# Weight stores moved to ScalarE's queue and a pair of token loads held back, in an attention and MoE kernel

## Chip, cores and metric

The kernel runs on one core of a Trainium2 chip. The metric is device time in microseconds (us) of one execution, taken as the median of several runs; lower is better. The engines are TensorE (PE; its weight loads are listed as PEld), VectorE (DVE), ScalarE (ACT), GpSimd (POOL) and SyncE (SP). DMAs are issued by an engine's own queue: SPq is SP's, ACTq is ACT's.

## The reference

```
scores = q @ k.T / 8 + bias(w1, b1, w2)        # 8 batches, 8 heads, 576 positions, 64 wide
attn = exp(scores - max) / (sum + 1e-9)
x = (attn @ v)  laid out as 4608 tokens x 512
a = x @ moe_w1 ; b = x @ moe_w2                # 512 -> 1024
out = ((a * b) @ moe_w3) @ moe_w_out           # 1024 -> 1024 -> 512
```

All is float32. The MoE matrices arrive as 64-bit floats, seen as pairs of 32-bit integers.

## The kernel before

**Stages.** First a table of position bias is made (L525 to L590), then 32 units of attention run (4 head pairs of 8 batches), then a MoE stage in which moe_w3 and moe_w_out are multiplied into one matrix (`fold`, L694) and the tokens go through six pairs of token blocks. A pair is 768 tokens, held as two column blocks c and d of 384. For each pair the hidden width 1024 is taken in 8 steps of 128 columns (the step is called ft or t).

**Precision.** Each operand is split into a high and a low part in a rounded format and a product is three matmuls: high by high, low by high, high by low.

**First pair and others.** For pair 0 a step multiplies plainly (`plain`, L788): 12 matmuls for a into PSUM tile X and 12 for b into PSUM tile Y, for column block c and then d. There is one X and one Y, so the next product has to wait until the old value is read. ScalarE copies X to SBUF (`gate` with "p", L806); VectorE multiplies Y by that copy (`gate` with "g", L809), which frees Y; both then split the result (L797, L800) and PE multiplies it by the folded matrix (`down`, L844). For the other pairs a scheme with seven products in place of eight is used (`product`, L774), with seven combined weight blocks per step.

**Weights.** Step t's weights are fetched in two halves (`fetch_w`; the DMA is L187, into a tile `wi` with two buffers, so a fetch waits until the one before the last was used up). The conversion is: ScalarE L195 and L199, VectorE L205, L209 and L219 (L219 frees `wi`), and POOL's integer sum L213, called the total below. Over eight steps these are 16 fetches. `sums_w` (L644, L647, L650) forms the combinations, `base_w` (L631, L633) splits the plain blocks; both write the tile `wS` (three buffers). At the end of `sums_w` the whole tile of 1792 KB is stored to DRAM (`w_d`, L652), to be loaded again for each later pair (`load_w`, L656).

**Tokens.** `load_x` fetches, for one half of a pair, two blocks `xr` (L711) and the softmax factors `rb` (L423), in many small DMAs. `split_x` multiplies the two (L734), forms differences (L737) and splits them (L742, L744) for pair 1 and later; `split_x0` does it for pair 0 (L722, L724, L726). `xr` and `rb` have one buffer each, so the loads of one half wait for the half before it.

**What sets the order.** From the MoE stage on, the order of PE, ACT, DVE and POOL is written out by hand: each step is put into a list `later` with a due time (in a model's microseconds), and `drive` emits the list in order of these times under a manual schedule for these four engines. SP's order is not in the list: a scheduler decides where each DMA of SP stands, by when it takes the DMA to be ready. Each engine and each queue works strictly in its order, so a DMA that waits holds back what stands behind it on the same queue.

Of the kernel before, what the change touches and what calls it, by code (L numbers as in the profile page):

```python
# [130 lines left out]
def relpos_attention_moe(  # L131
# [17 lines left out]
    nc = tc.nc  # L149
# [11 lines left out]
    def f(ap):  # L161
        return ap.bitcast(F32)
# [80 lines left out]
    def put(plan, steps, *times):  # L243

        def one():
            next(steps, None)
        for at in times:
            plan.append((at, len(plan), one))
# [111 lines left out]
    for i in range(2):  # L360
        t = att.enter_context(tc.tile_pool(name=f"sums{i}", bufs=1)).tile([P, 64], F32, name=f"sums{i}")
# [48 lines left out]
    def load_r(rb, p, rows, h, t0, t1):  # L410
        n = t0
        while n < t1:
            b, j = divmod(n, S)
            e = min(t1, b * S + (512 if j < 512 else S))
            o = rb[rows, n - t0:e - t0]
            if j < 512:
                j += b % 4 * 512
                src = r_m[p][b // 4, h:h + 1, j:j + e - n].broadcast_to([64, e - n])
            else:
                assert e - n == 64  # L420
                src = r_t[p][b // 4].rearrange("(h g b) j -> h b g j", h=2, g=2)[h:h + 1, b % 4].broadcast_to([64, 2, 32])
                o = o.rearrange("p (g j) -> p g j", g=2)
            nc.sync.dma_start(o, src)  # L423
            n = e
# [49 lines left out]
    later = []  # L474
# [5 lines left out]
    later = [e[:3] for e in later]  # L480

    plan = [e for e in later if e[0] < 0.0]
    later = [e for e in later if e[0] >= 0.0]
# [6 lines left out]
    with ExitStack() as pro:  # L490
# [29 lines left out]
        def reach(G):  # L520

            return (G + 1) * GR - 1, S - 1 - G * GR
# [9 lines left out]
        for G in range(NGRP):  # L532
            n = max(reach(G)) + 1
# [60 lines left out]
    later = [e for e in later if e[0] >= t_s]  # L594
# [4 lines left out]
    W2 = 2 * CH  # L599
# [10 lines left out]
    w_d = [dram.tile([P, 14 * 2 * P], F32, name=f"w_d{t}") for t in range(NF)]  # L610
# [5 lines left out]
    def fetch_w(t, m):  # L616

        if m == 0:
            big[t] = bg.tile([P, 4, 2 * P], F32, name="big")
        flat = big[t].rearrange("p s n -> p (s n)")  # L620
        src = (moe_w1, moe_w2)[m].rearrange("(c p) n -> p c n", p=P)[:, :, t * P:(t + 1) * P]
        for step in narrow(cva, src, NC * P, flat[:, m * NC * P:(m + 1) * NC * P], nc.sync, pieces=NC, signed=True):
            step()
            yield

    def base_w(t):
        x, w = big.pop(t), ups[0, t]
        w2 = bg.tile([P, 2, 2 * P], F32R, name="w2k", bufs=3)
        base[t] = (w[:, :, 0], w[:, :, 1], w2, w[:, :, 2])
        for o, y in ((w[:, :, 0:2], x[:, 0:2]), (w[:, :, 2], x[:, 3]), (w2, x[:, 2])):  # L630
            nc.scalar.activation(o[:, 0], y, AF.Copy)  # L631
            yield
            nc.vector.tensor_tensor(o[:, 1], y, f(o[:, 0]), op=ALU.subtract)  # L633
            yield

    def sums_w(t):
        x = big[t]
        w = ups[0, t] = wr.tile([P, 2, 7, 2 * P], F32R, name="wS")
        s = bg.tile([P, 4, 2 * P], F32, name="sums", bufs=1)
        for o, y, z, op in (  # L640
            (s[:, 0], x[:, 2], x[:, 3], ALU.add), (s[:, 2], x[:, 0], x[:, 2], ALU.subtract),
            (s[:, 1], s[:, 0], x[:, 0], ALU.subtract), (s[:, 3], x[:, 1], s[:, 1], ALU.subtract),
        ):
            nc.vector.tensor_tensor(o, y, z, op=op)  # L644
            yield
        for o in (0, 2):
            nc.scalar.activation(w[:, 0, 3 + o:5 + o], s[:, o:o + 2], AF.Copy)  # L647
            yield
        for o in (0, 2):
            nc.vector.tensor_tensor(w[:, 1, 3 + o:5 + o], s[:, o:o + 2], f(w[:, 0, 3 + o:5 + o]), op=ALU.subtract)  # L650
            yield
        nc.sync.dma_start(w_d[t], f(w.rearrange("p h s n -> p (h s n)")))  # L652

    def load_w(p, t):
        w = wr.tile([P, 2, 7, 2 * P], F32R, name="wS")
# [50 lines left out]
    def load_x(p, i, pool):  # L706
        xr = pool.tile([P, 8, CH], F32, name="xr")
        rb = pool.tile([P, 2, W2], F32, name="rb")
        flat = xr.rearrange("p s n -> p (s n)")
        for n, cc in enumerate((i, i + 2)):  # L710
            nc.sync.dma_start(flat[:, n * W2:(n + 1) * W2], x_d[cc][:, p * W2:(p + 1) * W2])  # L711
            for h, rows in enumerate((lo, hi)):
                load_r(rb[:, n], cc, rows, h, p * W2, (p + 1) * W2)
        return xr, rb, flat

    def split_x0(i):
        xr, rb, flat = load_x(0, i, (xs, xs1)[i])
        yield
        x = pairs[0]["x"][i] = x0p.tile([P, 2, 4, CH], F32R, name=f"xB{i}")
        for n in range(2):  # L720
            part, o = flat[:, n * W2:(n + 1) * W2], x[:, :, 2 * n:2 * n + 2].rearrange("p h s n -> p h (s n)")
            nc.vector.tensor_tensor(part, part, rb[:, n], op=ALU.mult)  # L722
            yield
            nc.scalar.activation(o[:, 0], part, AF.Copy)  # L724
            yield
            nc.vector.tensor_tensor(o[:, 1], part, f(o[:, 0]), op=ALU.subtract)  # L726
            yield

    def split_x(p, i):

        xr, rb, flat = load_x(p, i, xs)
        yield
        for n in range(2):
            nc.vector.tensor_tensor(flat[:, n * W2:(n + 1) * W2], flat[:, n * W2:(n + 1) * W2], rb[:, n], op=ALU.mult)  # L734
            yield
        for o, x, y in ((4, 1, 0), (6, 3, 1), (5, 3, 4), (7, 2, 5)):
            nc.vector.tensor_tensor(xr[:, o], xr[:, x], xr[:, y], op=ALU.subtract)  # L737
            yield
        x = xb[(p + 1) % 2].tile([P, 2, 7, CH], F32R, name=f"xS{i}")
        for s in range(7):  # L740
            src = xr[:, s + (s > 0)]
            nc.scalar.activation(x[:, 0, s], src, AF.Copy)  # L742
            yield
            nc.vector.tensor_tensor(x[:, 1, s], src, f(x[:, 0, s]), op=ALU.subtract)  # L744
            yield
        pairs[p]["x"][i] = x
# [128 lines left out]
    for i in range(2 * NF):  # L875
        hf, t = divmod(i, NF)
        t0 = t_f - (2 * NF - i) * PACE_F
# [15 lines left out]
    for t in range(NF):  # L893
        t0 = t_f + STEP0 * (t - 3) - LEAD_W * max(0, 3 - t)
        for m, (at0, d) in enumerate((((2.70, 3.35, 3.40, 3.80, 4.10, 4.90), -7.0), ((7.00, 7.65, 7.70, 8.00, 8.40, 9.40), -0.8))):
            size, rest, clamp, shift, mark, total = at0
            put(later, fetch_w(t, m), t0 + d, *(t0 + d for d in (size, rest, clamp, shift, mark, total)))
        t0 += STEP0
        put(later, base_w(t), *(t0 + d for d in (5.40, 6.00, 6.05, 6.55, 6.60, 7.00)))
        put(later, sums_w(t), *(t0 + 4.30 + 0.42 * d for d in range(4)), *(t0 + 9.70 + 0.65 * d for d in range(4)), t0 + 12.45)  # L900
    for i in range(2):
        t0 = t_s + AT_X0 + PACE_X0 * i
        put(later, split_x0(i), t0 - 5.0, *(t0 + d for d in (0.0, 1.1, 2.2, 3.3, 4.4, 5.5)))

    def start(n):
        return t_f + STEP0 * min(n, NF) + STEP * max(n - NF, 0)

    for n in range(NPR * NF):
        p, ft = divmod(n, NF)
        t0, t1 = start(n), start(n + 1)  # L910
        cs = dict(at=(p, ft))
        if p == 0:
            for j, u in AT_U.items():
                for m in range(2):
                    at(t0 + u + 2.08 * m, plain, cs, j, m)
                for k, d in AT_G.items():
                    if n == 0 and k + j == "gc":
                        d = AT_GC
# [18 lines left out]
        elif 0 < p < NPR - 1 and ft in (2, 5):  # L937
            i = int(ft > 4)
# [87 lines left out]
```

## Time and profile before

| what | value |
|---|---|
| median of 3 runs | 1067.21 us (1062.53 to 1070.43) |
| profiled execution | 1070.71 us, of which the span from first to last instruction is 1068.9 |
| PE busy | 1041.3 us, 97% of the span |
| PE weight loads | 828.4 us, 77% |
| DVE busy | 777.1 us, 73% |
| ACT busy | 559.9 us, 52% |
| POOL busy | 318.8 us, 30% |
| mean granted PE clock | 0.992 of full speed |

Times in the profile count from the start of the span. Busy time of PE includes its pipelining, so neighbouring matmuls overlap a little in the list. A releaser in brackets ("<-") is the engine and line whose end ended the idle time before an instruction.

### The profile page before, as it was taken

The page shows a single profiled execution, that of the slowest core. Times are in us where ns is not written, and L with a number is a line of the kernel's source. Part 1 is how long each engine was busy: PE and PEld are TensorE (multiplying, and loading weights), DVE is VectorE, ACT ScalarE, POOL GpSimd, SP SyncE. Part 2 cuts the span into 40 slices and gives each one's busy share as a digit, 9 for nine tenths or more (in the row PEclk, how much of TensorE's full clock was granted, in tenths as well). Part 3 has the DMA queues.
Part 4 walks back from the last instruction along what each step waited for, and adds up shares of the span by engine and source line. Part 5 has one row for each costly group of instructions (what it writes and reads, how often), then busy time and mean ns, then how long its engine had stood idle before and what let it go on. Part 6 is the DMA issues. An engine that isn't in the chain of part 4 may idle for free.

```text
span 1068.9 us, 33609 instructions
## 1 busy us (share of the span) xinstructions
PE 1041.3 (97%) x13968; PEld 828.4 (77%) x13968; DVE 777.1 (73%) x1478; ACT 559.9 (52%) x1277; POOL 318.8 (30%) x342
## 2 busy tenths in 40 slices
PE   7989999999999999999999999999999999999998
PEld 2346666666666666688899999999999999999997
DVE  8989999999999999998887455444635545453333
ACT  6957877886887778856543332323333232332222
POOL 0026885883788388674220000000000000000000
PEclk9979999999999999999999999999999999999999
DMA  7977777777776765367757765565575565545331
GB/s 218 297 237 207 205 199 215 221 213 198 207 223 189 208 190 168 112 175 245 261 197 274 255 220 195 198 246 197 181 262 188 190 234 214 196 183 214 139 138 59
DMA packets 97241, 218.37 MB, mean 204 GB/s; under 512 B 22592, under 2 KB 47296, under 8 KB 90944
## 3 DMA queue, kind: packets, MB, share of 16 engines
q1 hardware_dynamic: 96656, 216.19, 62.4%
q8 instruction: 110, 1.80, 0.7%
q14 instruction: 43, 0.35, 0.1%
q10 hardware_dynamic: 432, 0.02, 0.0%
HBM read 171.45 MB, written 44.71 MB: 202 GB/s over the span
## 4 chain that ended last, share of the span: by engine, by line
PE 79%; DVE 9%; issue 5%; DMA 3%; ACT 2%; SPq 2%; DVEq 0%; ACTq 0%
PE X L774 16%; PE acc L438 12%; PE Y L774 12%; PE s L342 11%; PE oc L844 9%; PE od L844 9%; DVE ts L353 4%; DVE pt L388 3%; PE bacc L562 3%; PE X L788 3%; PE Y L788 3%; DMA wi<-in_moe_w_dram 1%; SPq L423 1%; ACT pp L378 1%; DMA nb_d<-bev 1%
## 5 line engine op out<-in xcount | busy, mean ns | idle before, releaser
L438 PE MATMUL acc<-pt,v 32*64 32x128 f32 (+1 forms) x9216 | 215.4, 295 | 4.5 <-issue 4.3
L438 PEld LDWEIGHTS acc<-pt,v 32*64 32x64 f32 x9216 | 161.2, 131 | 72.8 <-issue 53.1
L378 ACT ACTIVATE pp<-ts,mx 128x576 f32<-128x576 f32 x256 | 196.0, 766 | 40.2 <-DVE mx L353 39.4
L342 PE MATMUL s<-k,q 64*128 64x288 f32 (+1 forms) x1280 | 196.3, 446 | 7.3 <-DVE mx L353 5.2
L774 PE MATMUL X<-xS,wS 128*128 128x384 f32 x960 | 194.9, 338 | 0.0
L353 DVE CUSTOM_DVE_ANT_0 ts<-s,nb 128x576 f32<-128x576 f32 x256 | 182.4, 738 | 7.2 <-PE s L342 7.1
L388 DVE STREAM_TRANSPOSE pt<-pp 128x1152 f32<-128x1152 f32 x128 | 175.5, 1373 | 3.0 <-ACT pp L378 2.5
L774 PEld LDWEIGHTS X<-xS,wS 128*128 128x128 f32 x960 | 171.4, 188 | 7.0 <-ACT wos L821 0.2
L342 PEld LDWEIGHTS s<-k,q 64*128 64x128 f32 (+1 forms) x1280 | 91.1, 177 | 77.0 <-issue 33.8
L817 DVE TENSOR_TENSOR wos<-X,wos 128x384 f32<-128x384 f32 x80 | 44.6, 558 | 138.7 <-PE X L774 138.7
L774 PE MATMUL Y<-xS,wS 128*128 128x384 f32 x720 | 145.0, 336 | 0.0
L774 PEld LDWEIGHTS Y<-xS,wS 128*128 128x128 f32 x720 | 127.9, 188 | 0.1
L330 POOL COPY v<-v 64x512 f32<-64x512 f32 (+1 forms) x160 | 87.6, 567 | 124.1 <-DMA v<-in_v_dram 109.2
L821 ACT COPY wos<-X 128x384 f32<-128x384 f32 x80 | 38.5, 481 | 126.1 <-PE X L774 126.1
L797 ACT ACTIVATE ghd<-wos 128x384 fp32r<-128x384 f32 x48 | 25.2, 525 | 125.4 <-DVE wos L817 105.7
L844 PE MATMUL oc<-w3s,ghc 128*128 128x512 f32 x288 | 89.8, 393 | 0.0
L844 PE MATMUL od<-w3s,ghd 128*128 128x512 f32 x288 | 89.6, 392 | 0.0
L817 DVE TENSOR_TENSOR wos<-Y,wos 128x384 f32<-128x384 f32 x80 | 44.6, 558 | 50.1 <-ACT wos L821 36.7
L225 POOL TENSOR_TENSOR wmag<-wmag 128x512 int32<-128x512 int32 x72 | 74.9, 1040 | 5.8
L797 ACT ACTIVATE ghc<-wos 128x384 fp32r<-128x384 f32 x48 | 25.2, 525 | 92.5 <-DVE wos L817 75.6
L844 PEld LDWEIGHTS oc<-w3s,ghc 128*128 128x128 f32 x288 | 53.4, 188 | 8.6
L844 PEld LDWEIGHTS od<-w3s,ghd 128*128 128x128 f32 x288 | 53.5, 188 | 8.5
(99 smaller groups left out, 1400.3 us busy)
## 6 DMA issues: line engine op xcount, KB each, us to landing
wS<-w_d SPq DMA_DIRECT2D x40, 1792.0 KB, 7.6
q<-in_q_dram SPq DMA_DIRECT2D x64, 288.0 KB, 4.3
w_d<-wS SPq DMA_DIRECT2D x8, 1792.0 KB, 6.5
v<-in_v_dram SPq DMA_DIRECT2D x96, 128.0 KB, 4.1
nb_d<-bev SPq DMA_DIRECT2D x36, 295.5 KB, 4.1
k<-in_k_dram SPq DMA_DIRECT2D x64, 144.0 KB, 4.0
x_d<-x SPq DMA_DIRECT2D x32, 288.0 KB, 3.8
xr<-x_d SPq DMA_DIRECT2D x24, 384.0 KB, 4.4
```

Source lines behind the costliest of these rows:

```text
L225: nc.gpsimd.tensor_tensor(d["bits"], d["bits"], d["bits"], op=ALU.add)
L330: nc.gpsimd.tensor_copy(t[64:128], t[0:64])
L342: nc.tensor.matmul(s[outs, hf, :HS], d[f"q{h}"][rows, q0:q0 + n], d[f"k{h}"][rows, :], start=True, stop=True,)
L353: nc.vector.tensor_tensor_reduce(out=halves(ts), in0=d.pop(("s", t))[:, :, :HS], in1=halves(NB[p, t]), op0=ALU.add, op1=ALU.min, scale=-1. ...
L378: nc.scalar.activation(d["p", ps][:, k * S:(k + 1) * S], ts, AF.Exp, bias=mx, scale=-1.0, accum_out=SUMS[u // 4 % 2][:, col:col + 1],)
L388: nc.vector.transpose(o, st[u].pop(("p", ts)))
L438: nc.tensor.matmul(acc[outs, a, c0:c0 + 32 * (t1 - t0)], d["v", b][rows, h], pt_[rows, t0:t1, 32 * b:32 * b + 32], start=(b == 0), stop=(b ...
L774: nc.tensor.matmul(acc, w[:, l, W_AT[n], i * P:(i + 1) * P], x[:, r, X_AT[n]], start=(k in "125" and i == 0 and m == 0), stop=(i == 1 and ...
L788: nc.tensor.matmul(acc, w[:, l, i * P:(i + 1) * P], x[:, r, 2 * k + "cd".index(j)], start=(n == 0), stop=(n == 11),)
L797: nc.scalar.activation(st[n], st["g" + j], AF.Copy)
L817: nc.vector.tensor_tensor(st[o], x, y, op=op)
L844: nc.tensor.matmul(d["o", j, t], l[:, sl], folded[ft][r], start=(ft == 0 and n == 0), stop=(ft == NF - 1 and n == 2),)
```

## The change

Three edits. The store of the split up weights is issued by ScalarE instead of SyncE. As ScalarE's order is written out by hand, the store's due time in `sums_w` now counts: it was t0 + 12.45 and becomes t0 + 19.50, 21.00 and 16.50 for step 0, step 1 and the later steps. And for the first half of pair 1 `load_x` has POOL clear two columns of `xr` and one column in 64 of `rb` before the loads are issued, so that each of these loads has to wait for POOL to reach this place in its order; the loads overwrite what was cleared.

```diff
-        nc.sync.dma_start(w_d[t], f(w.rearrange("p h s n -> p (h s n)")))
+        nc.scalar.dma_start(w_d[t], f(w.rearrange("p h s n -> p (h s n)")))
...
         flat = xr.rearrange("p s n -> p (s n)")
+        if (p, i) == (1, 0):
+            nc.gpsimd.memset(flat[:, 0:2 * W2:W2], 0.0)
+            nc.gpsimd.memset(rb.rearrange("p n (s j) -> p (n s) j", j=64)[:, :, 0:1], 0.0)
...
-        put(later, sums_w(t), *(t0 + 4.30 + 0.42 * d for d in range(4)), *(t0 + 9.70 + 0.65 * d for d in range(4)), t0 + 12.45)
+        put(later, sums_w(t), *(t0 + 4.30 + 0.42 * d for d in range(4)), *(t0 + 9.70 + 0.65 * d for d in range(4)), t0 + (19.50, 21.00, 16.50)[min(t, 2)])
```

Three lines are added at L710, so a line of the old kernel beyond it has a number three higher in the new one (L711 becomes L714, L806 becomes L809 and so on).

On SP's queue, at the start of pair 0's products, the old order is this (`wi` is a weight fetch, `xr` and `rb` from x_d_88, r_m_92 and r_t_96 belong to pair 1's first half, `w_d` is the store):

```order
L187 DMA wi<-in_moe_w_dram 128x4x256 x2
L711 DMA xr<-x_d_88 128x768
L652 DMA w_d_8994<-wS 128x3584
L187 DMA wi<-in_moe_w_dram 128x4x256
L423 DMA rb<-r_m_92 64x320
L423 DMA rb<-r_t_96 64x2x32
L423 DMA rb<-r_m_92 64x384
L423 DMA rb<-r_m_92 64x320
L187 DMA wi<-in_moe_w_dram 128x4x256
L652 DMA w_d_8995<-wS 128x3584
L187 DMA wi<-in_moe_w_dram 128x4x256
```

In the new order the same place of SP's queue reads:

```order
L187 DMA wi<-in_moe_w_dram 128x4x256 x12
L714 DMA xr<-x_d_88 128x768
L423 DMA rb<-r_m_92 64x320
L423 DMA rb<-r_t_96 64x2x32
L423 DMA rb<-r_m_92 64x384
L423 DMA rb<-r_m_92 64x320
L423 DMA rb<-r_t_96 64x2x32
L423 DMA rb<-r_m_92 64x384
L714 DMA xr<-x_d_90 128x768
```

The fourth to the fifteenth fetch now stand in one row, then come the two `xr` and twelve `rb` loads of pair 1's first half, then the sixteenth fetch. Further on, the weight load of pair 1's step 0 (L656), which stood behind the two `xr` loads of pair 1's second half, now stands ahead of them.

On ACT, around the second store (w_d_8995), the new order is as follows; `X` and `Y` are the PSUM tiles of pair 0, `wacc` those of the fold:

```order
L195 ACTIVATE wmag<-wi 128x512
L199 ACTIVATE big<-wi 128x512
L701 ACTIVATE w3s_1_9713<-wacc_9512 128x512
L652 DMA w_d_8995<-wS 128x3584
L631 ACTIVATE wS<-big 128x512
L701 ACTIVATE w3s_1_9723<-wacc_9516 128x512
L631 ACTIVATE wS<-big 128x256
L809 COPY wos_9741<-X 128x384
L631 ACTIVATE w2k<-big 128x256
L195 ACTIVATE wmag<-wi 128x512
```

The row with the DMA is new, the others stand as before. Eight such rows are added on ACT.

On POOL, near the end of its work, the new order is this; the row with x9 and the one with x3 are the last twelve totals of the weights:

```order
L683 TENSOR_TENSOR w3s_1_9529<-w3s_1_73,w3h 128x512
L683 TENSOR_TENSOR w3s_1_9556<-w3s_1_75,w3h 128x512
L213 TENSOR_TENSOR big<-big,wmag 128x512 x9
L711 MEMSET xr 128x2
L712 MEMSET rb 128x24
L213 TENSOR_TENSOR big<-big,wmag 128x512 x3
```

The two memsets stand behind the thirteenth of the sixteen totals. The orders of PE and DVE are unchanged.

## Rows read from the trace of the kernel before

**Rows 1.** What PE waited for: us in total, times, longest us.
```profile
PE X L788 <- ACT wos L806: 2.2, 1, 2.2
```
**Rows 2.** PE's timeline around 510: start us, us, engine, line, operation, count [idle before <-releaser].
```profile
510.00 3.81 PE L788 MATMUL X<-xB,wS 128*128 128x384 f32 x12 [2.22 <-ACT wos L806]
513.65 1.22 PE L788 MATMUL Y<-xB,w2k 128*128 128x384 f32 x6
```
**Rows 3.** Stretches of 2 us: us, busy of the engines, PEclk, DMA share, GB/s.
```profile
510.00:512.00 2.00, 2.00 (x6) 2.00 (x7) 2.00 (x5) 0.00 (x0) 0.00 (x0) 0.50 0.62 180
```
**Rows 4.** The chain that ended last, around 500 to 510: start us, us, what.
```profile
500.75 7.58 DMA wi<-in_moe_w_dram
...
509.58 0.38 ACT wos L806
```
**Rows 5.** ACT's timeline, 498 to 509.
```profile
498.81 0.63 ACT L631 ACTIVATE wS<-big 128x512 fp32r<-128x512 f32 x1 [1.23 <-POOL big L213]
...
502.13 0.42 ACT L631 ACTIVATE wS<-big 128x256 fp32r<-128x256 f32 x1 [2.20 <-POOL big L213]
...
508.36 0.67 ACT L195 ACTIVATE wmag<-wi 128x512 f32<-128x512 f32 x1 [1.40 <-DMA wi<-in_moe_w_dram]
```
**Rows 6.** The page's DMA issues: count, KB each, median us to landing.
```profile
wS<-w_d SPq DMA_DIRECT2D x40, 1792.0 KB, 7.6
...
w_d<-wS SPq DMA_DIRECT2D x8, 1792.0 KB, 6.5
```
**Rows 7.** DVE's timeline, 496 to 513.
```profile
496.94 2.39 DVE L650 TENSOR_TENSOR wS<-sums,wS 128x512 fp32r<-128x512 f32 x2
...
502.13 0.76 DVE L644 TENSOR_TENSOR sums<-big 128x256 f32<-128x256 f32 x2 [1.40 <-POOL big L213]
...
512.78 0.55 DVE L809 TENSOR_TENSOR wos<-Y,wos 128x384 f32<-128x384 f32 x1
```
**Rows 8.** All waits between 440 and 640, columns as in rows 1.
```profile
PEld Y L788 <- DVE wos L809: 0.3, 1, 0.3
```
**Rows 9.** SP's timeline at 499.
```profile
499.36 0.34 SPq L652 DMA_DIRECT2D w_d<-wS  x1
```
**Rows 10.** The instructions of L187, the weight fetches.
```profile
DMA to landing us min/median/max: 3.5/3.9/8.3
```
**Rows 11.** What SP's queue waited for between 440 and 640, columns as in rows 1.
```profile
SPq L187 <- DVE big L219: 35.0, 11, 5.4
```
**Rows 12.** Groups of POOL's instructions: busy us, mean ns | idle before.
```profile
L362 POOL MEMSET sums<- 128x64 f32 x2 | 0.2, 152 | 0.3 <-POOLq L1011 0.3
```
**Rows 13.** POOL's timeline at 541.
```profile
541.75 1.28 POOL L213 TENSOR_TENSOR big<-big,wmag 128x512 int32<-128x512 int32 x1 [5.47 <-DVE big L219]
```
**Rows 14.** SP's timeline, 564 to 573.
```profile
564.05 1.24 SPq L423 DMA_DIRECT2D rb<-r_m  x2
...
572.60 1.65 SPq L711 DMA_DIRECT2D xr<-x_d  x2
```
**Rows 15.** ACT's timeline, 552 to 558.
```profile
552.55 0.66 ACT L199 ACTIVATE big<-wi 128x512 f32<-128x512 uint32 x1
...
557.05 0.67 ACT L195 ACTIVATE wmag<-wi 128x512 f32<-128x512 f32 x1
```
**Rows 16.** DVE's timeline, 558 to 582.
```profile
558.56 0.42 DVE L205 TENSOR_SCALAR wmag<-wmag 128x512 f32<-128x512 f32 x1
...
562.80 0.55 DVE L809 TENSOR_TENSOR wos<-Y,wos 128x384 f32<-128x384 f32 x1
...
581.64 1.82 DVE L734 TENSOR_TENSOR xr<-xr,rb 128x768 f32<-128x768 f32 x2
```
**Rows 17.** PE's timeline, 561 to 564.
```profile
561.79 2.28 PE L788 MATMUL X<-xB,wS 128*128 128x384 f32 x12
563.91 1.21 PE L788 MATMUL Y<-xB,w2k 128*128 128x384 f32 x6
```
**Rows 18.** The chain that ended last, at 589; columns as in rows 4.
```profile
589.19 2.11 PE Y L788 x12
```

## The prediction

> **What bounds the kernel now.** I read the list of what TensorE waits for first, since PE is busy for 97% of the span: what can be won is what it waits. Its longest entries belong to the bias and attention stages, which the change does not touch. The MoE stage has one: the plain product into PSUM tile X waits 2.2 us for ScalarE's copy at L806 [rows 1]. Then I looked that place up in PE's own timeline. X starts at 510.00 after 2.22 us of idleness and takes 3.81 us for 12 matmuls [rows 2]; the same 12 take 2.28 us elsewhere [rows 17], so another 1.53 us goes after the wait. The stretch table says why: the granted clock is 0.50, the lower level of 1.2 GHz, in 510 to 512 [rows 3], right after PE had stood still. So 2.22 + 1.53 = 3.75 us is all that this place can give, 0.35% of the run.
>
> The chain of waits says who holds L806 back: the weight fetch issued at 500.75 takes 7.58 us, two ScalarE conversions wait for it, and the copy, which stands behind them in ScalarE's order, ends at 509.96 [rows 4]. ScalarE's timeline has the same as 1.40 us of idleness ahead of the conversion at 508.36 [rows 5]. A usual weight fetch lands in 3.9 us [rows 10]. This one (the eighth of sixteen) stands in SP's queue directly behind the store of split up weights that left at 499.36 [rows 9], and a store takes 6.5 us [rows 6]. So the slow fetch is the store's doing.
>
> Last I asked what PE would meet next, and this decides the forecast. After X comes Y, at 513.65 [rows 2]. It needs VectorE's L809, which reads the old Y out of PSUM. L809 stands at 512.78 and ends at 513.33 [rows 7]; the wait list has a weight load of Y waiting 0.3 us for it [rows 8]. VectorE has no idle time at all between the L644 at 502.13, which waited for POOL, and the end of L809 [rows 7]. So L809 is late by VectorE's own work, and an earlier weight fetch does not move it.
>
> **The change part by part.**
>
> *The stores leave from ScalarE.* Eight DMA issues go from SP to ACT. The same store takes SP 0.34 us to issue [rows 9]; for ACT I take 0.4 each, 3.2 us in all. The seven other than store 1 stand, by the order, just ahead of an instruction that idles for POOL, PE or VectorE, or between two that do, and ACT is busy for 52% only. Bounds: 0, and 0.4 for one that finds no idle time; I take 0.
>
> Store 1 matters. It may not leave before VectorE's L650 has written the last of its data: 496.94 + 2.39 = 499.33 [rows 7]. ACT reaches the new place after an L701 and idles there before L631 anyway; it would now wait until 499.33, issue, and start L631 at about 499.75, not 498.81 [rows 5]: 0.94 later. Queued behind it on ACT are L701, L631 and the first L806. The next L631 waits 2.20 us for POOL until 502.13 [rows 5], so the 0.94 is swallowed before anything PE wants. Bounds: 0 to 0.94; I take 0.
>
> The point is that store 1 leaves at the same moment as before (499.36 then, about 499.4 now), 1.3 us ahead of the eighth fetch, which still waits for the same VectorE instruction to free its buffer. Only the queue is another one. What two queues do to each other the trace does not show, since every large transfer of before is on SP's queue. Bounds from rows: unhindered, the fetch lands at 500.75 + 3.9 = 504.65; hindered as now, at 508.33. A slower landing than now I exclude to within some tenths, for no bytes are added.
>
> By the Trainium skill (DMA: Bandwidth & Descriptors, Issuing engines are not separate DMA queues) the queues of all issuing engines run on the same 16 DMA engines, and a second issuer saves only issue time; the same page (Queues, rings and completion order) lets each engine take turns between queues packet by packet. No run here shows two loaded queues. By the first the landing stays near 508.3 and the sum here is 0; by turns in equal bytes it comes forward and the sum is that of the first rival.
>
> Take either end. If nothing changes, PE resumes X at 510.00 as before. If the fetch lands early, ACT is free at 508.36 - 1.40 = 506.96, and its chain of 1.60 us (508.36 to 509.96) ends at 508.56. X then runs from 508.6 to 510.9, and Y still waits for 513.33. Y starts 513.65 - 513.35 = 0.3 us earlier than before. So this part gives 0 to 0.3 us, not 3.75. I take 0.2.
>
> *SP's queue without the stores.* All fetches from the 4th to the 15th now stand in a row. In the old run SP waited 35.0 us in eleven of these fetches for VectorE's L219 [rows 11], which frees the buffer, so they were not late by what stood ahead of them and don't move. 0.
>
> *The loads of the second pair held back.* Two POOL memsets of 2 and 24 columns: 0.15 us each by the nearest row [rows 12], on an engine that idled 5.47 us before the 13th total [rows 13]. They stand behind this total, which ends at 541.75 + 1.28 = 543.03. Two xr and twelve rb loads follow on SP at 0.64 us each (1.24 us for two and the gaps) [rows 14]: 543.3 + 14 x 0.64 = 552.3. VectorE first needs them behind the L205 of 558.56 [rows 16]. The sixteenth weight fetch now stands behind these fourteen, leaves at 552.3 and lands at 556.2 with the usual 3.9 us. ACT wants it at 557.05 [rows 15]. So 0, with 0.85 us in hand before anyone waits. If this cover goes, see the second rival.
>
> *The second half of the pair.* Its two xr loads left at 572.60 [rows 14]; now a weight load of 7.6 us [rows 6] stands ahead in SP's queue. At worst they come 7.6 us later, at 572.60 + 7.6 + 3.9 = 584.1 if the 3.9 us of a 512 KB fetch [rows 10] stand for one of 384 KB, against a first use at 581.64: 2.5 us late. The two products would end at 583.46 + 2.5 = 586.0 and the L809 behind them (0.55) at 586.5 [rows 16]; PE wants its Y at 589.19 [rows 18]. So 2.7 us stay in hand: 0.
>
> **Sum.** -0.2 (Y) and nothing else: the profiled execution's 1070.71 becomes 1070.5. The three times of before are 1062.53 to 1070.43 with median 1067.21; the profiled one lies 3.5 above it. On the median's footing the forecast is 1067.0. A difference of 1% (10.7 us) is about what a measurement of this kernel tells from no change, and the runs themselves spread by 8 us, so this counts as no change.
>
> **Rivals.**
>
> *The wait moves from X to Y and takes the slow clock with it* (slightly slower). If the fetch lands early, PE idles 0.8 us ahead of X and about 2.4 us ahead of Y. The row shows a fall to 0.50 after 2.22 us of idleness; the same after Y's wait costs 1.53. X no longer pays its 1.53, and Y starts 0.3 earlier: net -0.3 + 1.5 = +1.2, so 1068.4. For it: the same length of wait. Against: it needs the two queues to share well.
>
> *The sixteenth fetch comes late* (slower). Place: PE's Y at 563.91 [rows 17]. The fetch leaves at 552.3 and store 5 leaves ACT right behind the fifteenth conversion, which ended at 552.55 + 0.66 = 553.2 [rows 15]: they run side by side. The slowest fetch beside a store took 8.3 us [rows 10]: landing at 560.6. Slack: ACT's L195 would end 557.72 and VectorE's L205 started at 558.56 [rows 15, 16], 0.84; L809 ended 563.35 and Y began 563.91 [rows 16, 17], 0.56. So from a landing after 557.05 + 1.40 = 558.45 on PE waits, at 8.3 us for 2.15 us, plus 1.53 if the clock falls: +3.7, so 1070.9. For it: fourteen issues ahead. Against: this fetch leaves some 0.9 us ahead of the store, the slow ones left behind it.
>
> *The whole 3.75 us goes* (faster): 1063.5. This needs VectorE to bring L809 forward by 3 us. For it: ACT and DMA are freer. Against: VectorE has no gap to close before L809.
>
> *The change doesn't do what it says*: a store that leaves at the same moment and a queue that shares badly give exactly the old trace, 1067.2. It falls together with the forecast.
>
> **Chances.** No change to within a microsecond, 0.50; the wait moves to Y, 0.22; the late sixteenth fetch, 0.15; the whole gain, 0.08; a stall of over 10 us among the reordered loads, for which no row speaks, 0.04; rounding 0.01. Range: from the whole gain at 1063.5 to the late fetch at 1070.9, widened by about 1.3 us on each side because three runs of the same kernel already spread by 8: 1062.2 to 1072.2. Faster by over 1% would need more than every wait PE has in this stage: 0.02. Slower by over 1%: 0.04. Within: 0.94.
>
> **What would show it.** Right: the fetches from the 4th on leave at VectorE's pace; store 1 leaves at about 499.4; L809 ends near 513.3 and Y starts within 0.3 us of it; after that PE waits for nothing; xr loads leave near 543 and the sixteenth fetch lands before 558. Wrong: L809 several microseconds earlier (the whole gain was there), a new PE wait near 564 or 589 (late loads), or a landing of the eighth fetch later than 508.3.

## The result and the profile after

The changed kernel takes 1073.96 us (median of 12 runs, 1071.30 to 1078.20), the kernel before 1067.57 us on the same chips (12 runs, 1062.53 to 1071.43). The ratio is 1.0053, with a 95% interval of 1.0037 to 1.0069: slower by 5.7 us (4.0 to 7.4). That is within 1%, but above the range of the prediction, which ended at 1072.2.

The profiled execution after took 1071.4 us with a span of 1069.5, only 0.7 us more than the profiled one of before. To compare the two one has to go by stages. First the source views of the last attention product, of the plain product and of the product of the later pairs, of the kernel before:

```profile
L438 PE MATMUL acc<-pt,v x9216: 264/294/522, 69.5 to 456.8; 32*64 32x160 f32 x99, 32*64 32x128 f32 x98
L788 PE MATMUL X<-xB,wS x192: 332/338/688, 498.9 to 595.1; 128*128 128x384 f32 x192
L774 PE MATMUL X<-xS,wS x960: 333/337/444, 600.5 to 1060.4; 128*128 128x384 f32 x192
L774 PE MATMUL Y<-xS,wS x720: 333/334/346, 599.5 to 1057.2; 128*128 128x384 f32 x180
```

And the same of the changed kernel:

```profile
L438 PE MATMUL acc<-pt,v x9216: 264/294/523, 68.7 to 452.4; 32*64 32x160 f32 x102, 32*64 32x128 f32 x95
L791 PE MATMUL X<-xB,wS x192: 334/338/446, 494.4 to 595.8; 128*128 128x384 f32 x192
L777 PE MATMUL X<-xS,wS x960: 332/337/346, 601.2 to 1061.0; 128*128 128x384 f32 x192
L777 PE MATMUL Y<-xS,wS x720: 333/334/444, 600.1 to 1057.8; 128*128 128x384 f32 x180
```

"a to b" is the first and last start. The attention, which the change doesn't touch, ended 4.4 us earlier in this execution (452.4 against 456.8; over the runs of this study it ends between 450.7 and 457.9), and this hides the loss. The stage of pair 0, from the first plain product to the first product of pair 1, grew from 599.5 - 498.9 = 100.6 us to 600.1 - 494.4 = 105.7 us: 5.1 us. The five pairs behind it take 1060.4 - 599.5 = 460.9 us before and 1061.0 - 600.1 = 460.9 after. So the loss is in the stage of pair 0, and 5.1 fits the measured 5.7 (4.0 to 7.4).

What PE waited for between 440 and 1080, where before had 2.2 us in one wait [rows 1] and a weight load of 0.3 [rows 8]:

```profile
PE Y L791 <- DVE wos L812: 4.4, 3, 1.5
PE X L791 <- ACT wos L809: 3.0, 2, 1.7
```

Five waits stand at three places. The first is the one that the change was aimed at [rows 2]; PE's timeline there:

```profile
502.39 1.22 PE L791 MATMUL Y<-xB,wS 128*128 128x384 f32 x6
505.30 2.38 PE L791 MATMUL X<-xB,wS 128*128 128x384 f32 x12 [1.68 <-ACT wos L809]
509.22 1.32 PE L791 MATMUL Y<-xB,w2k 128*128 128x384 f32 x6 [1.54 <-DVE wos L812]
```

The X wait is shorter (1.68 against 2.22), its 12 matmuls no longer run at half clock (2.38 against 3.81), and Y waits 1.54 instead. VectorE's timeline says for what, as [rows 7] did:

```profile
497.96 0.76 DVE L644 TENSOR_TENSOR sums<-big 128x256 f32<-128x256 f32 x2 [1.41 <-POOL big L213]
...
508.63 0.54 DVE L812 TENSOR_TENSOR wos<-Y,wos 128x384 f32<-128x384 f32 x1
```

Between these two rows VectorE has no idle time. L812 ends at 509.17, and Y starts at 509.22. In the kernel before the last products into the old Y stand here:

```profile
506.55 1.23 PE L788 MATMUL Y<-xB,wS 128*128 128x384 f32 x6
```

From there to the new Y at 513.65 [rows 2] it was 7.10 us. Now it is 509.22 - 502.39 = 6.83: 0.27 us less.

The second and third places are new. PE's timeline at both, with an undisturbed product in the last two rows:

```profile
557.23 0.39 PE L847 MATMUL od<-w3s,gld 128*128 128x512 f32 x1
558.93 2.38 PE L791 MATMUL X<-xB,wS 128*128 128x384 f32 x12 [1.32 <-ACT wos L809]
562.82 1.31 PE L791 MATMUL Y<-xB,w2k 128*128 128x384 f32 x6 [1.51 <-DVE wos L812]
...
565.03 0.63 PE L847 MATMUL oc<-w3s,ghc 128*128 128x512 f32 x2
...
585.92 2.28 PE L791 MATMUL X<-xB,wS 128*128 128x384 f32 x12
589.54 1.34 PE L791 MATMUL Y<-xB,w2k 128*128 128x384 f32 x6 [1.33 <-DVE wos L812]
...
591.77 0.63 PE L847 MATMUL oc<-w3s,ghc 128*128 128x512 f32 x2
...
593.83 2.28 PE L791 MATMUL X<-xB,wS 128*128 128x384 f32 x12
...
598.05 0.63 PE L847 MATMUL od<-w3s,ghd 128*128 128x512 f32 x2
```

Undisturbed, X and Y together take 598.05 - 593.83 = 4.22 us. At the third place they take 591.77 - 585.92 = 5.85, 1.63 more. At the second they take 565.03 - 558.93 = 6.10, 1.88 more, and X itself starts 558.93 - 557.46 = 1.47 late (an undisturbed product follows the last row of `down`, here the one at 557.23, by 0.23): 3.35 in all. 3.35 + 1.63 = 4.98 of the 5.1 us. The brackets alone (2.83 and 1.33) are less, since the matmuls behind a wait overlap less, too.

The chain that ended last names both causes:

```profile
549.35 7.91 DMA wi<-in_moe_w_dram
557.29 0.67 ACT wmag L195
...
573.88 13.31 DMA xr<-x_d
```

The first is the sixteenth weight fetch, the second the token load of pair 1's second half.

### The profile page after: what moved, and what is told of

Read it like the earlier page. It is cut to its first block, busy times and chain, and to the rows that moved or that the text cites. A ratio compares the mean times of both kernels' runs of the same rounds, so it can differ in the third digit from the quotient of the medians.

```text
span 1069.5 us, 33610 instructions
## 1 busy us (share of the span) xinstructions
PE 1040.2 (97%) x13968; PEld 825.8 (77%) x13968; DVE 775.4 (72%) x1478; ACT 559.3 (52%) x1277; POOL 318.3 (30%) x344
## 4 chain that ended last, share of the span: by engine, by line
PE 71%; DVE 12%; issue 8%; DMA 3%; ACT 2%; POOL 2%; DVEq 0%; SPq 0%; ACTq 0%; POOLq 0%
PE X L777 16%; PE Y L777 12%; PE acc L438 11%; PE s L342 10%; PE oc L847 9%; PE od L847 9%; DVE ts L353 5%; DVE pt L388 3%; PE bacc L562 3%; POOL w3s L683 2%; PE Y L791 2%; PE X L791 1%; DMA xr<-x_d 1%; DMA wi<-in_moe_w_dram 1%; DMA nb<-nb_d 1%
## 5 line engine op out<-in xcount | busy, mean ns | idle before, releaser
L438 PE MATMUL acc<-pt,v 32*64 32x160 f32 (+1 forms) x9216 | 213.6, 295 | 3.3 <-issue 3.3
```

The costliest lines, as they stand in the source:

```text
L438: nc.tensor.matmul(acc[outs, a, c0:c0 + 32 * (t1 - t0)], d["v", b][rows, h], pt_[rows, t0:t1, 32 * b:32 * b + 32], start=(b == 0), stop=(b ...
```

## The experiments

All are compared with the kernel before, which ran on the same chips. "Stage" is the stage of pair 0 as above (100.6 before, 105.7 after), "pairs" the five behind it (460.9 both), each from the one profiled execution; the ratios are from the timed runs. A difference of 0.6 us between two stages need not come from an edit: in e1, e3, e4, e5, e6 and e9 PE also waits some 0.6 us for X about 5 us into the stage, and in e6 the orders of PE, ACT, DVE and POOL up to there are those of the kernel before.

| run | ratio (95% interval) | in us | stage | pairs |
|---|---|---|---|---|
| e1_stores_only | 1.0012 (0.9995 to 1.0029) | +1.3 | 102.2 | 460.9 |
| e2_hold_only | 0.9998 (0.9980 to 1.0016) | -0.2 | 100.6 | 460.8 |
| e3_fetch16_act | 1.0022 (1.0000 to 1.0045) | +2.4 | 102.3 | 460.9 |
| e10_store5_later | 1.0009 (0.9994 to 1.0024) | +1.0 | 102.4 | 460.8 |
| e4_store7_late | 1.0073 (1.0047 to 1.0099) | +7.8 | 104.7 | 466.1 |
| e5_both_loads | 1.0025 (1.0007 to 1.0043) | +2.7 | 101.4 | 461.7 |
| e6_store1_behind | 1.0011 (0.9992 to 1.0030) | +1.2 | 103.0 | 460.8 |
| e7_l809_ahead | 0.9982 (0.9963 to 1.0002) | -1.9 | 99.4 | 460.9 |
| e8_all | 0.9992 (0.9973 to 1.0011) | -0.9 | 99.7 | 462.3 |
| e9_two_stores | 0.9976 (0.9960 to 0.9993) | -2.6 | 101.1 | 460.7 |

### Which part of the change costs the time

The theory (T1) was that the late sixteenth fetch costs most of it, and that it takes both parts: the held back loads ahead of it in SP's queue and a store that ScalarE issues at the same moment. e1 is the changed kernel without the memsets:

```diff
-        if (p, i) == (1, 0):
-            nc.gpsimd.memset(flat[:, 0:2 * W2:W2], 0.0)
-            nc.gpsimd.memset(rb.rearrange("p n (s j) -> p (n s) j", j=64)[:, :, 0:1], 0.0)
```

> The changed kernel without POOL's two memsets: the stores leave from ScalarE at their new places, the first half's loads are free again (SP issues them early). Theory 1, late loads: the loss of the changed kernel is two loads that come late, the sixteenth weight fetch (PE waits of 1.32 ahead of X and 1.51 ahead of Y) and the two xr loads of the second half (1.33 ahead of Y). Here no loads stand ahead of the sixteenth fetch, but the weight load still stands ahead of the two xr loads, so only 1.3 us of waits remain: +1 to +2 us against before. Theory 2, the stores on ScalarE's queue cost the time by themselves: +6. Theory 3, holding the loads back costs it by itself: 0.

e2 is the kernel before with these lines added, its stores still on SP.

> The kernel before with POOL's two memsets alone: the stores stay on SP at their old due time. SP's order has the fourteen loads ahead of the sixteenth fetch as in the changed kernel, but store 5 behind that fetch and the old order of the two xr loads. Theory 1, late loads: the fetch leaves as late as in the changed kernel but has no store to share with, lands in about 4 us and is just in time: 0 to +1 us. Theory 2, stores: 0. Theory 3, holding: +6.

Both came out as theory 1 said. Neither part alone loses what both lose together: +1.3 and -0.2 against +5.7; by stages +1.6 and 0.0 against +5.1. In e1 the fetch left at 542.41, ahead of its store (546.66), and PE has no wait at the second place; the third is there with 0.67. In e2 the fetch stands behind the fourteen loads and the store behind the fetch, both on SP:

```profile
551.09 0.53 SPq L187 DMA_DIRECT2D wi<-in_moe_w_dram  x1
551.72 0.45 SPq L652 DMA_DIRECT2D w_d<-wS  x1
```

ScalarE uses the fetch at 556.04 without waiting for it, and PE waits at the first place only (X 1.71, Y 1.50).

### The second place: who is ahead of whom

e3 issues the sixteenth fetch from ScalarE, past the loads; e10 leaves it behind the loads and moves only the store of step 5 behind it.

```diff
 e3:  narrow(cva, src, ...,
-    nc.sync, pieces=NC, signed=True)
+    nc.scalar if (t, m) == (7, 1) else nc.sync, pieces=NC, signed=True)
 e10: due time of the store of step t
-    t0 + (19.50, 21.00, 16.50)[min(t, 2)]
+    t0 + (19.50, 21.00, 16.50, 16.50, 16.50, 21.50, 16.50, 16.50)[t]
```

> The changed kernel with the sixteenth weight fetch issued by ScalarE, so that it no longer stands behind the fourteen loads. Theory 1, late loads: the two waits of 1.32 and 1.51 us go, about 3 us less than the changed kernel: +2.5 to +3.5 against before. Theories 2 and 3: +6 as the changed kernel.

> The changed kernel with the store of step 5 alone due 21.50 in place of 16.50, so that it leaves behind the sixteenth weight fetch; the fourteen loads still stand ahead of this fetch. If the fetch was late because the store had left just ahead of it (theory), it lands in 4 to 5 us, PE's waits of 1.32 and 1.51 us near 559 to 563 go, those near 589 (xr, 1.34) stay: plain stage 102 to 103 us (105.7 in the changed kernel), time 2.5 to 3.5 us above the kernel before. If the fourteen small loads alone made it late (rival), the waits stay: 105 to 106 us, 5 to 6 us above before.

Both took the second place away, and the stage fell by 3.4 and 3.3 us (the place had cost 3.35; so close a match is partly luck, since the other places changed a little as well). e10 tells which of the two causes decides. SP's and ScalarE's timelines in it:

```profile
554.76 0.53 SPq L187 DMA_DIRECT2D wi<-in_moe_w_dram  x1
```

```profile
558.66 0.67 ACT L195 ACTIVATE wmag<-wi 128x512 f32<-128x512 f32 x1 [0.61 <-DMA wi<-in_moe_w_dram]
558.87 0.33 ACTq L652 DMA_DIRECT2D w_d<-wS  x1
```

With the fourteen loads still ahead of it, the fetch is used 3.9 us after its issue, the store leaves behind it, and PE does not wait. So the loads made the fetch late only as far as they let a store pass in front; the store did the rest. The stage is as long as expected; that the third place went as well (PE's Y is 0.3 us late there, 0.76 in e3) was given back at the first, where the granted clock fell to 0.50 behind Y in this execution. The time of +1.0 (-0.6 to 2.6) is below the expected 2.5 to 3.5; the stage's +1.8 lies within its interval.

### The third place: token loads beside a store and a weight load

e4 takes the changed kernel and delays the store of step 7 (due 24.00, not 16.50), so that it leaves behind the token loads. e5 adds to e3 that the first weight load of pair 1 is issued by ScalarE behind this store, and so no longer ahead of the token loads.

```diff
 e5:
-        nc.sync.dma_start(f(w.rearrange("p h s n -> p (h s n)")), w_d[t])
+        (nc.scalar if (p, t) == (1, 0) else nc.sync).dma_start(f(w.rearrange("p h s n -> p (h s n)")), w_d[t])
...
-            put(later, load_w(p, ft), t0 - 2 * STEP + 0.3)
+            put(later, load_w(p, ft), t0 - 2 * STEP + (4.5 if (p, ft) == (1, 0) else 0.3))
```

> The changed kernel with the last store's due time 7.5 later, so that it no longer shares the DMA engines with the two xr loads of the second half. Theory 1, late loads: xr lands near 582 to 584 and not 587, the wait of 1.33 us ahead of Y goes: about 1.5 us less than the changed kernel, +4.5 to +5 against before. If the weight load ahead on SP's queue is what holds xr and not the store beside it, xr stays near 587 and nothing changes: +6. Theories 2 and 3: +6.

> The changed kernel with the sixteenth fetch issued by ScalarE and, besides, the weight load of pair 1's first step issued by ScalarE behind the last store, so that it no longer stands ahead of the two xr loads. Theory 1, late loads: both late loads are in time, PE's waits near 560 and 589 are gone and the stage from the first plain product to the first product of pair 1, which took 100.6 us before and 105.7 in the changed kernel, takes 100.5 to 101; the time is within 1 us of before. Rival: the store beside xr is what delays it, not the weight load ahead; then xr still comes near 586 and the stage stays at 102.

The third wait went in both. VectorE's L737, the first use of xr, in e4 and then in e5 (6.45 us of waiting in the changed kernel):

```profile
584.19 1.83 DVE L737 TENSOR_TENSOR xr<-xr,rb 128x768 f32<-128x768 f32 x2 [1.02 <-DMA xr<-x_d]
```

```profile
580.85 1.82 DVE L737 TENSOR_TENSOR xr<-xr,rb 128x768 f32<-128x768 f32 x2
```

PE waits at neither. So it takes the store and the weight load together to make xr late; without either one it comes in time. But both runs pushed a transfer into the next pair. In e4 the store landed 13.5 us after its issue at 588.34 (6.8 is usual), VectorE waited 4.03 us for a store of the output, PE 3.45 us behind it at 617.09, and the pairs took 5.2 us more: +7.8, a miss where +4.5 to +5 was expected. In e5 the pairs lost 0.8 and the stage was 101.4, not 100.5 to 101; at +2.7 (0.7 to 4.6) the time missed its "within 1 us", too.

### The first place: who holds Y

e6 is the kernel before with store 1 alone issued by ScalarE, late enough (due 27.50) to let the eighth fetch go first. It is the case that the first rival asked for: this fetch unhindered.

> The kernel before with store 1 alone on ScalarE, at a place behind the eighth fetch, so that this fetch has no store ahead of it. The prediction: the eighth fetch lands in some 4 us, PE's wait ahead of X shrinks to 0.8 us or less, and Y starts no earlier than 0.3 us, since VectorE's L809 does not move; the wait ahead of Y grows to 2.5 to 3 us. Time within 1 us of before, or 1.5 slower if the clock falls. Rival, the whole wait goes: Y starts some 3 us earlier, -3 us.

PE's and VectorE's timeline, and the stretch behind the wait (us, busy of the engines, PEclk, DMA share, GB/s):

```profile
505.74 2.38 PE L788 MATMUL X<-xB,wS 128*128 128x384 f32 x12 [0.69 <-ACT wos L806]
510.76 2.22 PE L788 MATMUL Y<-xB,w2k 128*128 128x384 f32 x6 [2.65 <-DVE wos L809]
```

```profile
510.16 0.55 DVE L809 TENSOR_TENSOR wos<-Y,wos 128x384 f32<-128x384 f32 x1
```

```profile
512.00:514.00 2.00, 2.00 (x8) 2.00 (x7) 1.47 (x4) 0.77 (x2) 0.12 (x1) 0.50 1.15 387
```

X comes early, Y waits 2.65 us for L809, which VectorE reaches without idling since 499.37, and the granted clock falls to 0.50, the lower level of 1.2 GHz. The stage is 2.4 us longer than before. So the eighth fetch is not what bounds this place.

e7 attacks what does: the kernel before with VectorE's L809 emitted ahead of the two L650 and the conversions of the next fetch (and ScalarE's L806 with it), the DMAs unchanged:

```diff
-                    at(t0 + u + 2.08 * m, plain, cs, j, m)
+                    at(t0 + (4.00 + 1.50 * m if (n, j) == (0, "d") else u + 2.08 * m), plain, cs, j, m)
...
+                    if n == 0 and j == "d" and k in "pg":
+                        d = {"p": 6.10, "g": 6.85}[k] - u
```

> The kernel before with ScalarE's copy of X and VectorE's L809 of the first step's second block put ahead of VectorE's two L650 and three L205, L219, L209, and ahead of ScalarE's conversions of the eighth fetch. Nothing else moves. If VectorE's own order bounds Y, L809 ends some 2.4 us earlier, PE's two waits shrink to about 0.9 us in all, the stage takes about 98 us and not 100.6: -2 to -2.7 us. If the late fetch bounds it: 0.

The stage is 99.4, 1.2 us shorter; the waits left are Y 1.03 at 506.65 and X 0.99 at 518.35. The time is -1.9 us, with an interval that just includes 0, so the timed runs alone don't show a gain. Both the stage and the waits fell short of what was expected (98 us, 0.9 us in all). By the stage, a reordered VectorE gives here what a fetch without hindrance (e6) did not.

### Looking for a version that beats both

e8 is the changed kernel with the repairs of e5 and the reordering of e7. e9 is e7 with the stores of steps 1 and 2 issued by ScalarE behind the fetches that they held up.

> The changed kernel with all three repairs (sixteenth fetch on ScalarE, weight load behind the xr loads, L809 ahead). Theory 1 and VectorE's order together: as the kernel before with L809 ahead, -2 to -2.7 us against before, so about 8 us faster than the changed kernel. If moving the stores had a use of its own, more than that.

> The kernel before with VectorE's L809 ahead (as in e7_l809_ahead) and only the stores of steps 1 and 2 issued by ScalarE, each behind the weight fetch that it used to hold up (due 27.50 and 16.50); the other six stay on SP. If the two remaining waits of e7 (Y 1.03 us, X 0.99 us) come from fetches that land behind a store, both go: the plain stage is 98 to 99 us long (99.4 in e7, 100.6 before) and the time is 2 to 3 us below the kernel before. If a fetch beside a store that was issued after it is slowed as well, the waits stay at 1 us each and the time is that of e7, 0.5 to 1.5 us below before. The pairs behind stay at 461 us under both.

e8 gains 0.9 us by stage and loses 1.4 in the pairs: no change, where -2 to -2.7 was expected. e9 is the only kernel whose interval lies below 1 (-2.6 us, -4.3 to -0.7), but its profile doesn't bear out the reason for it: with its stage at 101.1 us it still waits for X 1.94 at 525.03, where ScalarE waits 3.11 us for the tenth fetch, and Y 1.02 at 512.33. Store 2 left at 513.50, before that fetch could (514.90), so moving the stores only changed which fetch lands behind one. Its profiled execution (1071.67) is also the slowest of its twelve. Whether e9 is better than e7 stays open.

## Why the prediction was wrong, step by step

**Right: Y is bound by VectorE.** The forecast gave the first place 0 to 0.3 us, not 3.75; it gained 0.27, L809 was as late as before (from the L644 behind POOL to the end of L809 11.20 us then, 11.21 now), and e6 showed the same with the fetch unhindered. Store 1 left 1.4 us ahead of the eighth fetch, as before though from another queue, and the fetch was still slow: ScalarE waited 0.86 us for it, 1.40 before [rows 5].

**Right in part: the first rival.** The wait did move in part from X to Y. That it takes the lower clock along held in e6 (2.65 us) but not in the changed kernel (1.54 us, clock 1.00 behind it). Nor was it two queues that share well that moved it: e2, whose stores all stay on SP, has the same waits and the same 512.53 - 505.71 = 6.82 us:

```profile
505.71 1.22 PE L791 MATMUL Y<-xB,wS 128*128 128x384 f32 x6
508.64 2.39 PE L791 MATMUL X<-xB,wS 128*128 128x384 f32 x12 [1.71 <-ACT wos L809]
512.53 1.33 PE L791 MATMUL Y<-xB,w2k 128*128 128x384 f32 x6 [1.50 <-DVE wos L812]
```

What e2 shares with the changed kernel are the held back loads, which SP issued right behind the eighth fetch in the kernel before (from 501.17 on). That these loads slowed the fetch there, by some 0.5 us, is likely but rests on one execution of each.

**Wrong: "The sixteenth weight fetch ... leaves at 552.3 and lands at 556.2 ... So 0, with 0.85 us in hand".** The term was 14 x 0.64 us of issuing = 9.0. SP's timeline after shows 549.35 - 538.77 = 10.6 for the same fourteen loads, since some took 1.0 to 1.4 (e2, with the stores on SP, has just the 9.0: 551.09 - 542.11; so the sum fitted the loads, and it is with the stores on ScalarE that issuing them took longer, for a reason that no run shows):

```profile
538.77 0.34 SPq L714 DMA_DIRECT2D xr<-x_d  x1
539.17 1.13 SPq L423 DMA_DIRECT2D rb<-r_m  x1
...
549.35 0.53 SPq L187 DMA_DIRECT2D wi<-in_moe_w_dram  x1
```

And ScalarE's:

```profile
548.77 0.35 ACTq L652 DMA_DIRECT2D w_d<-wS  x1
...
557.29 0.66 ACT L195 ACTIVATE wmag<-wi 128x512 f32<-128x512 f32 x1 [4.48 <-DMA wi<-in_moe_w_dram]
```

The error of 1.6 us would have cost nothing by itself. But the second rival was judged by an order: "this fetch leaves some 0.9 us ahead of the store". It left 0.6 us behind it, and landed after 7.9 us, near the 8.3 that the rival used. So the rival came true: it foresaw 2.15 us of waiting for Y there, and the waits measured 1.32 + 1.51 = 2.83 us, for X as well. That its price of 3.7 us comes near the 3.35 of this place is partly luck: 1.53 of it were for a lower clock, and the granted clock stayed at 1.00. An order that hangs on 0.9 us was treated as known, from a sum that had an error of nearly twice that.

**Wrong: "So 2.7 us stay in hand: 0" for the second half's tokens.** At worst they were to come 7.6 + 3.9 = 11.5 us after 572.60. SP's, VectorE's and ScalarE's rows after:

```profile
572.87 0.50 SPq L656 DMA_DIRECT2D wS<-w_d  x1
573.47 0.84 SPq L714 DMA_DIRECT2D xr<-x_d  x2
```

```profile
587.19 1.83 DVE L737 TENSOR_TENSOR xr<-xr,rb 128x768 f32<-128x768 f32 x2 [6.45 <-DMA xr<-x_d]
```

```profile
575.82 0.33 ACTq L652 DMA_DIRECT2D w_d<-wS  x1
```

Two sizes were off. Measured to the place where PE wants Y (589.19 before; 588.21 without the wait after), the issue at 573.88 is 14.3 us ahead where 16.6 was reckoned: all twelve rb loads of this half now stood ahead of it on SP's queue, where eight did before, and some took 1.3 to 1.4 us to issue. And the landing took 13.3, not 11.5, because it had both the weight load ahead on its own queue and store 7 beside it; the bound had only the first. 2.3 + 1.8 = 4.1 us, more than the 2.7 in hand, and 1.33 us of waiting is what is left of it. e5, which moves the weight load behind, took the wait away, and so did e4, which moves the store. In the range, too, one late load was the worst case (1070.9, and 1.3 on top); two came late, 3.35 + 1.63 us.

**Left out: what SP's one order had protected.** The part on SP's queue without the stores asked only whether the fetches would leave earlier, and there its 0 holds. But both new waits come with a store that is issued from a queue where nothing orders it against the loads on SP's (the second needs the weight load ahead besides). In the old kernel store 5 stood behind the sixteenth fetch by SP's order, as e2 still has it; with two queues nothing kept this order. The late fetch had a chance of 0.15 in the forecast and the tokens none.

## What to carry to other kernels

Before a DMA is given to another queue, list which loads the old queue's order put ahead of it, and ask for each whether it still leaves first; if that hangs on less than the error of the sum, count it as lost. A stall with two resources behind it (here the late fetch for X, VectorE's own work for Y) is worth only what is left when the second one is reached, and the order of the second engine (e7) can be the cheaper thing to move. A transfer that is pushed out of one stage has to be looked for in the next: e4 won its wait in the stage and lost 5.2 us behind it.

## What was not expected of the hardware

How two loaded queues share could not be seen before. It can be now, and it came out in two ways. The queues' packets, MB and share of the 16 DMA engines in the changed kernel, first in the 5.5 us in which store 1 (on q10) ran and the eighth fetch, which SP had issued at 496.6, should have run as well:

```profile
q10 hardware_dynamic: 128, 1.84, 94.5%
q1 hardware_dynamic: 101, 0.09, 4.7%
```

then from 501.0 to 503.6:

```profile
q1 hardware_dynamic: 528, 0.52, 58.6%
...
q10 hardware_dynamic: 16, 0.00, 0.3%
```

A fetch is 0.5 MB, so all of it ran after the store had ended, as if both were on one queue; in e2, where they are on one, it was used 7.1 us after its issue, the same as here. The sixteenth fetch fared alike: from 549.3 to 555.2 store 5 moved 1.84 MB and SP's queue 0.16 MB in all, and from 555.2 on SP's queue moved 0.52 MB. But from 581 to 588, with the token loads and the next weight load on q1 and store 7 on q10, both ran at once:

```profile
q10 hardware_dynamic: 128, 1.61, 53.7%
q1 hardware_dynamic: 317, 1.26, 49.0%
```

The store was shared with, and so were the tokens: store 7 landed after 11.3 us (6.8 usual), xr after up to 13.9 (4.8 usual). By the Trainium skill (DMA: Bandwidth & Descriptors, Queues, rings and completion order) the engines take turns between queues packet by packet. The last stretch agrees with that; the first one doesn't: from 497.2 to 501.0 no packet of SP's queue ran at all, and why stays open. Even with turns the fetch would have come late: the store's 128 packets would have let by about as many of the fetch's 500 or so (an estimate from these counts).

The clock is the other point. The granted clock fell to 0.50 behind waits of 2.22 us (before), 2.65 (e6), 3.45 (e4) and 1.75 (Y in e10, with 1.47 us of X's wait 4 us ahead of it), but stayed at 1.00 behind X waits of 1.87 in e1 and 1.94 in e9, behind 1.69 in e3 (Y, with 1.52 of X 4 us ahead of it), and behind all five waits of the changed kernel. The length of one wait does not settle it.
